# A Mamba-2 scan and a SwiGLU network in one kernel: block 0's scan in chunks of 64, block 1's decays from stored sums, a new order of steps

## The chip, the cores and the metric

The kernel runs on one core of one Trainium2 chip. Its metric is the time of one execution on the device in microseconds (us). The engines are TensorE (PE, with its weight loads PEld), VectorE (DVE), ScalarE (ACT), GpSimd (POOL) and SyncE (SP), which here issues nearly all DMAs.

## What is computed

The reference has two parts. The first is a Mamba-2 scan over x (4 batches, 8 heads, 768 positions, head dimension 32) with decays a and with B and C (state dimension 16). The second is a normed SwiGLU network without biases on the 3072 tokens with 256 features each (model dimension 256, hidden dimension 1536). Cut to what matters:

```
for each chunk of positions:
    cum = cumsum(log(clip(a)))                       # within the chunk
    L   = exp(cum_i - cum_j) for j <= i, else 0
    y   = ((C B^T) * L) x  +  exp(cum) * (C state)
    state = exp(sum log a) * state + sum_j exp(cum_last - cum_j) B_j x_j
X  = y as tokens x 256
xn = X / sqrt(mean(X^2) + 1e-6) * rms_g
out = (silu(xn w_gate) * (xn w_val)) w_out
```

The result of the scan does not depend on the size of a chunk, so a kernel may choose it. The three weight matrices arrive as 64-bit floats; the kernel loads their 16-bit words and makes 32-bit floats of them itself.

## The kernel before

The 3072 tokens are worked in six blocks of 512 (block 0 to 5). A block is two pairs p of two stretches of 128 positions, so blocks 0, 1 and 2 hold the pairs 0 to 1, 2 to 3 and 4 to 5. While TensorE computes the network for one block, the other engines prepare the scan of the next one.

All work is written as small steps, and one string, `order` (line 1269), lists them: `0:gate.2/1` is step gate with the number 2 for block 0, in the PSUM slot 1; a step named `1:S.0` belongs to the table for the later blocks, and acts on the block after the one named (or on the one after that). The list is run through once when the kernel is built, and each step issues its instructions to its engine's queue. So the list is, for each engine by itself, the order in which it works; between engines only the data and the release of buffers order them. DMAs are issued by SP in the same way, each step's DMAs in SP's own order.

The steps that this document speaks of:

- Setup: constants and masks by VectorE and GpSimd (`ident`, `never`, `mid`, `middles` and more, lines 279 to 375); `idle` (line 325), products on zeros at the very start; `bc` and `x` load B, C and x; `aT`, `la0`, `log` turn a and take its logarithms; `c`, `cx`, `ch`, `cc` (lines 426 to 442) make each chunk's whole decay, `d`, `dx` (lines 410 to 420) the decays to and from a chunk's ends.
- Decays L inside a chunk, way one, on TensorE: `mask` (line 457) puts a large negative number above the diagonal, `sums` (line 464) adds differences of sums of logs by small products out of `r` and `parts` (lines 386 to 403: the sums split in three 16-bit parts on VectorE), and `exp` (line 486) takes exponentials. Way two, by loads: `row`, `rowout` (lines 1143 to 1154) store rows of sums in DRAM, `spread` (line 496) loads each row to 64 partitions (128 KB a load), `sub`/`subp` (line 503) subtracts the token's own sum on VectorE/GpSimd, `ex` (line 510) takes exponentials and masks what lies above the diagonal on GpSimd (`causal`, line 491).
- Scores: `turn`, `T`, `Tt`, `Td`, `last` transpose B and C, `g` or `gg` (lines 586 to 616) multiply them, `L` and `L1` (lines 623 to 644) multiply scores by decays on VectorE.
- States: `A` (line 656) adds up B times x on TensorE; `S` (line 671) masks that sum and steps the state from chunk to chunk on VectorE.
- Outputs: `y` (lines 695 and 726) on TensorE; `yt` (line 791) takes them out of PSUM, `sq` (line 769), `ms`, `rs`, `rb`, `xn` (lines 812 to 842) norm them.
- Weights: 18 pieces, `fetch` (line 171) loads one, `pow` (two passes on ScalarE, line 210), `man` and `wt` (VectorE, lines 221 and 227) convert it; six pieces at a time have a buffer.
- Network of block 0: hidden columns 0 and 1 before the norm is known (`early`, line 869, then `norm`, line 882), 2 to 5 by `gate` (line 860), `silu` and `hid`; the rest, and all of the later blocks, by a scheme of fewer products of combined operands: `P` (line 933; seven product steps k for each j), `take`, `C`, `silu`, `hid` (lines 955 to 974), with `cw` and `tx` (lines 909 and 922) for the combinations. The output projection is `o` in block 0 and `O` (line 1060) with `u` and `w` later; `put` stores.

In this kernel block 0 is scanned in chunks of 128 (way one, in four halves `mask.0.0` to `mask.1.1`), and with two output steps `y.0` and `y.1`, one for each pair. Block 1 is scanned in chunks of 64, its decays by way one too (`mask.2`, `mask.3`), its scores with `gg.2` and `gg.3` and its outputs with `y.2` and `y.3`. Blocks 2 to 5 have chunks of 64, decays by way two, one score step, and two output steps each.

PSUM has two pairs of banks for the wide results of blocks 0 and 1 (slots 0 and 1, which `switch` gives to the later pools), a third pair (slot 2) and two single banks (`bank`, line 92). A step that takes a slot waits until the last reader of what was in it is done.

Of the kernel before, what the change touches and what calls it, by code (L numbers as in the profile page):

```python
# [9 lines left out]
FP32 = mybir.dt.float32  # L10
# [10 lines left out]
def kernel(  # L21
# [92 lines left out]
    def load(p, queues=(nc.sync, nc.sync)):  # L114
        br = raw.tile([P, 2, NH, N], FP32, tag="br", name="br")
        st.setdefault(p, {}).update(B=br)
        if p < 4:
            st[p]["C"] = raw.tile([P, 2, NH, N], FP32, tag="cr", name="cr")
        for i, queue in enumerate(queues):
            load_chunk(p, i, queue)  # L120
# [18 lines left out]
    def load_chunk(p, i, queue=nc.sync):  # L139
        b, c0 = divmod(2 * p, NC)  # L140
        sl = slice((c0 + i) * P, (c0 + i + 1) * P)
        for name, src in (("B", B), ("C", C))[0:2 if p < 4 else 1]:
            queue.dma_start(out=st[p][name][:, i], in_=src[b, :, sl, :].rearrange("h s n -> s h n"))

    def load_x(p, queue=nc.sync):
        b, c0 = divmod(2 * p, NC)
        st.setdefault(p, {})["x"] = raw.tile([P, 2, NH, D], FP32, tag="xr", name="xr")
        for i in range(2):
            sl = slice((c0 + i) * P, (c0 + i + 1) * P)
            queue.dma_start(out=st[p]["x"][:, i], in_=x[b, :, sl, :].rearrange("h s n -> s h n"))  # L150
# [59 lines left out]
    def power(k):  # L210
        top, below, dst, shape = fetched[k]
        n = shape[1] * shape[2]
        e = cvt.tile([P, n], FP32, tag="e", name="e", bufs=4)
        g = e.rearrange("p (a b) -> p a b", a=shape[1])
        activation(out=g, in_=top, func=AF.Prelu, scale=-1.0, bias=kinks[:, 0:1],
                   alpha=2.0 ** -40)
        activation(out=g.bitcast(I32), in_=g, func=AF.Prelu, scale=-2.0 ** 59,
                   bias=kinks[:, 1:2], alpha=2.0 ** -40)
        parts[k, "e"] = g.bitcast(I32)
# [7 lines left out]
    def weight(k):  # L227
        top, below, dst, shape = fetched[k]
        e, f = parts.pop((k, "e")), parts.pop((k, "f"))
        nc.vector.tensor_tensor(out=dst.bitcast(I32), in0=f, in1=e, op=ALU.bitwise_or)  # L230
# [13 lines left out]
    later_part = const.tile([P, 1], FP32, name="later_part")  # L244
    third_part = const.tile([P, 1], FP32, name="third_part")
    three = const.tile([P, 1], FP32, name="three")
    head = const.tile([P, NH], FP32, name="head")
    sel = const.tile([P, NH], BF16, name="sel")
    ident16 = const.tile([P, P], BF16, name="ident16")
    whole16 = const.tile([P, P], BF16, name="whole16")  # L250
# [3 lines left out]
    eps = const.tile([P, 1], FP32, name="eps")  # L254
# [3 lines left out]
    NG = 2 * NC * NB + 4  # L258
# [4 lines left out]
    la4 = [early_ones[:, 256 + k * P:256 + (k + 1) * P].rearrange("p (q k h) -> p q k h", q=4, k=4)  # L263
           for k in range(2)]
    mids = const.tile([P, 2, P], FP32, name="mids")
    mid = mids[:, 0]
    first_four = slice(0, 4), slice(0, NH)
# [11 lines left out]
    def whole_chunks():  # L279
        nc.vector.memset(chunk_ones, 0.0)  # L280
        for u, r in enumerate(halves):
            nc.vector.memset(chunk_ones[r, u], 1.0)
# [12 lines left out]
    def of_quarters():  # L295
        nc.vector.tensor_scalar(out=three, in0=part[:, 3:4], scalar1=-1.0, scalar2=1.0,
                                op0=ALU.mult, op1=ALU.add)
        nc.vector.tensor_scalar_add(later_part, part[:, 0:1], -1.0)
        nc.vector.tensor_scalar(out=third_part, in0=part[:, 2:3], scalar1=-1.0, scalar2=None,
                                op0=ALU.mult)  # L300
# [4 lines left out]
    def from_middle():  # L305
        nc.vector.tensor_copy(out=mid, in_=upto)
        nc.vector.tensor_scalar_add(mid[0:HC], mid[0:HC], -1.0)

    def from_middles():
        nc.gpsimd.tensor_copy(out=mid, in_=upto)  # L310
        for r in halves:
            half_of = slice(r.start, r.start + HC // 2)
            nc.gpsimd.tensor_scalar(out=mid[half_of, r], in0=mid[half_of, r], scalar1=-1.0,
                                    scalar2=None, op0=ALU.add)
        minus_mid()

    def mask16():
        for r in halves:
            nc.vector.tensor_copy(out=never16[r], in_=never[r, r])

    def kinks_of_powers():
        for k, v in enumerate((-14336.0, -28672.0 * 2.0 ** 19)):
            nc.vector.memset(kinks[:, k:k + 1], v)
# [18 lines left out]
    def logs_again(g, n):  # L342
        b, c = divmod(g, NC)
        activation(
            out=la4[g // 4][:, g % 4:g % 4 + n],
            in_=la0[:, c:c + n, b * NH:(b + 1) * NH].unsqueeze(2).to_broadcast([P, n, 4, NH]),
            func=AF.Ln)

    def minus_mid():
        nc.gpsimd.tensor_scalar(out=mids[:, 1], in0=mid, scalar1=-1.0, scalar2=None,  # L350
                                op0=ALU.mult)
# [16 lines left out]
        "mid": from_middle, "middles": from_middles,  # L368
        "never16": mask16, "ident16": lambda: nc.vector.tensor_copy(out=ident16, in_=ident),
        "whole16": lambda: nc.vector.tensor_copy(out=whole16, in_=never),  # L370
# [5 lines left out]
        "log": lambda: activation(out=la, in_=la0, func=AF.Ln), "mids": minus_mid,  # L376
# [133 lines left out]
    def exponential(g):  # L510
        L = pair_tile(g)
        activation(out=L, in_=L, func=AF.Exp)
        causal(L)
# [965 lines left out]
```

## Time and profile before

| | us |
|---|---|
| median of 3 runs (388.93 to 391.95) | 389.05 |
| the profiled execution | 389.76 |
| its span, from the first to the last instruction | 388.0 |
| TensorE busy in the span | 382.5 |
| VectorE, ScalarE, GpSimd busy | 277.8, 214.3, 150.1 |
| moved by DMA | 28.04 MB |

The profile is of one execution. Its span starts with the first instruction, and all times in the document count from there. A row of the timeline gives start, duration, engine, line of the kernel, operation and operands with their shapes, and how many like it follow each other; matmuls are pipelined, so the duration of one is longer than the distance to the next one. A 32-bit product is two rows. A row of the groups gives busy us, the mean ns of one instruction, and the idle time before them with what ended it.

### The profile page before, as it was taken

To read this page: it belongs to the slowest core of one execution; us is meant where nothing else is said; L and a number is where in the kernel's file an instruction comes from. 1 tells how busy PE (TensorE), PEld (TensorE's weight loads), DVE (VectorE), ACT (ScalarE), POOL (GpSimd) and SP (SyncE) were. 2 spreads that over 40 slices of the span, in tenths; PEclk is the share of its full clock that TensorE was granted. 3 is DMA by queue.
4 is the path that set the end of the run, shared out by engine and by line. 5 is a ranking of instruction groups with operands and counts; after the bars stand their busy time and mean duration, and the time that the engine had idled before them with its cause. 6 is when DMAs were issued, how large, how long until landed. Compare 5 with 4: busy or idle time off the path is not lost.

```text
span 388.0 us, 9604 instructions
## 1 busy us (share of the span) xinstructions
PE 382.5 (99%) x3805; PEld 330.0 (85%) x3805; DVE 277.8 (72%) x593; ACT 214.3 (55%) x453; POOL 150.1 (39%) x168
## 2 busy tenths in 40 slices
PE   8999999999999999999999999999999999999996
PEld 5676488888888999888899988899888899988995
DVE  6896979876967988669594766868374677454684
ACT  2878677956867272675864244753344571345420
POOL 5022045503693365243568601355611235212231
PEclk9999999999999999999999999999999999999999
DMA  8888988483073404634336112000100001000001
GB/s 91 236 128 233 311 169 179 124 166 30 3 101 87 52 11 96 144 42 100 65 75 85 27 42 42 2 18 19 56 3 2 2 14 48 29 1 0 2 0 56
DMA packets 109940, 28.04 MB, mean 72 GB/s; under 512 B 94824, under 2 KB 107848, under 8 KB 109896
## 3 DMA queue, kind: packets, MB, share of 16 engines
q1 hardware_dynamic: 107816, 27.30, 33.9%
q8 instruction: 30, 0.49, 0.6%
q10 hardware_dynamic: 2080, 0.13, 0.4%
q14 instruction: 14, 0.11, 0.1%
HBM read 23.68 MB, written 3.74 MB: 71 GB/s over the span
## 4 chain that ended last, share of the span: by engine, by line
PE 97%; DVE 1%; ACT 1%; issue 0%; ACTq 0%; DVEq 0%
PE gate L951 29%; PE o L1072 23%; PE val L951 22%; PE o L983 5%; PE gate L865 4%; PE y L736 3%; PE gate L875 2%; PE g L599 2%; PE e L460 1%; PE g L592 1%; PE y L664 1%; PE tp L540 1%; PE e L474 0%; DVE ob L1103 0%; PE idle L328 0%
## 5 line engine op out<-in xcount | busy, mean ns | idle before, releaser
L963 DVE TENSOR_TENSOR c<-val,p 128x512 f32<-128x512 f32 x99 | 67.3, 686 | 49.4 <-PE val L951 35.2
L957 ACT COPY p<-gate 128x512 f32<-128x512 f32 x99 | 56.8, 581 | 61.6 <-PE gate L951 59.3
L951 PE MATMUL gate<-tx,wgv 128*128 128x256 f32 x264 | 65.8, 381 | 0.0
L208 ACT ACTIVATE c<-c 128x256 f32<-128x256 f32 x99 | 40.0, 415 | 39.2 <-DVE c L963 38.9
L976 POOL TENSOR_TENSOR hid<-c 128x256 f32<-128x256 f32 x31 | 23.8, 769 | 89.6 <-ACT c L208 84.9
L951 PEld LDWEIGHTS gate<-tx,wgv 128*128 128x128 f32 x264 | 49.3, 190 | 6.9 <-ACT p L957 0.2
L1103 DVE TENSOR_TENSOR ob<-ob,o 128x128 f32<-128x128 f32 (+1 forms) x90 | 24.2, 297 | 21.7 <-PE o L1072 16.9
L976 DVE TENSOR_TENSOR hid<-c 128x256 f32<-128x256 f32 x68 | 34.0, 513 | 6.7 <-ACT c L208 6.6
L1072 PE MATMUL o<-two,hid 128*128 128x128 f32 x280 | 36.5, 276 | 0.1
L1072 PEld LDWEIGHTS o<-two,hid 128*128 128x128 f32 x280 | 34.5, 192 | 1.1 <-DVE hid L976 0.4
L951 PE MATMUL val<-xn,wgv 128*128 128x256 f32 x132 | 33.7, 381 | 0.0
L951 PE MATMUL val<-tx,sw 128*128 128x256 f32 x132 | 33.5, 380 | 0.0
L951 PE MATMUL val<-xn,sw 128*128 128x256 f32 x132 | 33.3, 381 | 0.0
L951 PE MATMUL gate<-tx,sw 128*128 128x256 f32 x132 | 33.0, 380 | 0.0
L951 PE MATMUL gate<-xn,wgv 128*128 128x256 f32 x132 | 32.7, 380 | 0.0
L493 POOL TENSOR_SCALAR_AFFINE_SELECT L<-L 64x512 f32<-64x512 f32 x32 | 22.8, 713 | 18.1 <-ACT L L208 16.8
L951 PEld LDWEIGHTS val<-xn,wgv 128*128 128x128 f32 x132 | 24.8, 190 | 3.5
L951 PEld LDWEIGHTS val<-tx,sw 128*128 128x128 f32 x132 | 24.9, 190 | 3.4 <-issue 0.2
L951 PEld LDWEIGHTS gate<-tx,sw 128*128 128x128 f32 x132 | 24.8, 190 | 3.4 <-issue 0.2
L951 PEld LDWEIGHTS val<-xn,sw 128*128 128x128 f32 x132 | 24.4, 190 | 3.2 <-issue 0.2
L951 PEld LDWEIGHTS gate<-xn,wgv 128*128 128x128 f32 x132 | 24.4, 190 | 3.1
L208 ACT ACTIVATE u<-gate 128x256 f32<-128x256 f32 (+1 forms) x37 | 14.6, 402 | 18.2 <-PE gate L951 15.3
(202 smaller groups left out, 702.6 us busy)
## 6 DMA issues: line engine op xcount, KB each, us to landing
L<-rowd SPq DMA_DIRECT2D x32, 128.0 KB, 3.3
xr<-in_x_dram SPq DMA_DIRECT2D x24, 128.0 KB, 3.6
out_dram<-ob SPq DMA_DIRECT2D x24, 128.0 KB, 2.4
wr<-in_moe_w_out_dram SPq DMA_DIRECT2D x6, 511.5 KB, 6.3
wr<-in_moe_w_gate_dram SPq DMA_DIRECT2D x5, 511.5 KB, 5.4
wr<-in_moe_w_val_dram SPq DMA_DIRECT2D x5, 511.5 KB
br<-in_B_dram SPq DMA_DIRECT2D x23, 64.0 KB, 2.6
dT<-rowe SPq DMA_DIRECT2D x10, 128.0 KB
```

Of the source, the lines that this page charges most:

```text
L208: nc.scalar.activation(**operands)
L493: nc.gpsimd.affine_select(out=L[r], in_=L[r], pattern=[[0, L.shape[1]], [1, HC]], compare_op=ALU.is_ge, fill=0.0, base=0, channel_multipli ...
L599: nc.tensor.matmul(out=g[u, P * i:P * i + P].rearrange("p (t m) -> p t m", t=2), lhsT=T[r, i, 0, u], rhs=T[r, i, 1:3, u], start=(first and ...
L736: nc.tensor.matmul(out=y[2 * k + u][rows, (2 * n + i) * HC:(2 * n + i + 1) * HC], start=(k, u, rows.start) not in opened, stop=True, skip_ ...
L865: nc.tensor.matmul(out=gv[:, k], lhsT=w[:, t, fs], rhs=xns[0][:, t], start=(t == 0), stop=(t == 1))
L951: nc.tensor.matmul(out=dst[:, half[w]], lhsT=lhsT, rhs=rhs, start=(k in (1, 2, 5) and w == 0), stop=True, skip_group_check=True)
L957: nc.scalar.copy(out=t, in_=Xs[j])
L963: nc.vector.tensor_tensor(out=t, in0=Zs[j], in1=a, op=ALU.add)
L976: engine.tensor_tensor(out=hid[:, 2 * j + c // 10 - 1, c % 10 - 1], in0=u, in1=src[:, half[1]], op=ALU.mult)
L983: nc.tensor.matmul(out=o, lhsT=hid[:, f, k // 2, (k % 2) * P:(k % 2 + 1) * P], rhs=wo[:, f], start=opens, stop=(f == NF - 1), skip_group_c ...
L1072: nc.tensor.matmul(out=Os[blk, b][:, place * P:(place + 1) * P], lhsT=hidden_or_sum(u)[:, g], rhs=rhs, start=(blk, b) not in opened, stop= ...
L1103: nc.vector.tensor_tensor(out=o, in0=o, in1=src, op=ALU.add if what[0] == "+" else ALU.subtract)
```

## The change

Three things change together.

First, block 0 is scanned in chunks of 64 like the rest. Its decays still come from TensorE, but with the narrow masks and sums that block 1 had (`mask.0`, `mask.1`, `sums.0`, `sums.1`); its scores are one step (`g.0`), its state sums are one step for both pairs (`AA.0`), with `Sn` to mask them and seven states instead of four, and its outputs are one step, `y.0`. All later blocks too have one output step in place of two, with the state sums for the next block behind it:

```
-    def outputs(p, pair, after, n=0):
+    def outputs(blk, pair):
...
+        def between():
+            for j in range(4):
...
+        def within():
+            for j in range(4):
...
+        if blk == 0:
+            within()
+            between()
+        else:
+            between()
...
+            within()
+            if blk + 1 < NBLK:
+                next_additions()
```

Second, block 1's decays come by way two: `spread.4` to `spread.7` in two loads each (one for each half of the partitions), `subp` on GpSimd, `ex`, and `ca` for the mask. `mask.2`, `mask.3`, their sums, `r.1` and `parts.1` go away, and so do the wide mask, the sums over all 128 positions in `d` and `c`, and the two filler products ahead of `c`:

```
-            for u in range(2):
-                n = sum(v == u for i, v in chunks)
...
+    def spread(g, u):
         b, c = divmod(g, NC)
         o = (c * BH + b * NH) * HC
...
+        r = halves[u]
+        nc.sync.dma_start(out=pair_tile(g)[r].rearrange("p h m -> p (h m)"),
+                          in_=rowv[u, o:o + NH * HC].partition_broadcast(HC))
```

Third, many steps are cut finer (`pow` in its two passes, `parts` in four, `norm`, `xn`, `sq`, `yt`, `rs`, `middles`), B and C share five buffers in place of three each, x has four in place of three, and the whole list is in a new order. The parts of the new list that the prediction speaks of, the steps of one stretch as they stand there:

```
0:idle.7 ... 0:mask.0/0 0:sel 0:middles.0 0:bc.0 0:x.0 0:aT ... 0:la0 0:log ... 0:turn.0 0:Tb.0 0:T.0
0:c/2 0:r.0 0:row.1 0:parts.0.0 0:cx 0:mask.1/1 0:fetch.1 0:rowout.1 0:rowe.1 0:d 0:dx 0:tok 0:tokout
0:turn.1 0:T.1 0:parts.0.1 0:ch 0:cc 0:parts.0.2 0:parts.0.3 0:sums.1 0:exp.1 0:x.1 ... 0:Tb.1 0:fetch.0
...
0:spread.4.1 0:spread.5.1 0:spread.5.0 0:fetch.3 0:fetch.2 0:bc.2 0:sums.0 0:exp.0 0:g.0/2 0:L1.0.3
0:L1.0.2 0:L.0 0:last.1 0:pow.1.0 0:Tl.1 0:AA.0/0 0:Sn.0.0 0:Sn.0.1 0:S.0.0 ... 0:S.0.6 0:y.0/1
...
0:early.0.1/0 0:early.0.0 ... 0:ms.0 0:rs.0.0 0:rs.0.1 0:wt.3 0:xn.0.1 0:xn.0.0 0:turn.2 0:T.2 0:Tt.2.0
0:norm.0.0 0:tx.0.2 0:subp.4 0:ca.5.1 0:pow.2.1 0:early.1.0/2 0:ex.4 0:ca.4.1 0:ca.4.0 0:bc.3 0:scale.3
0:early.1.1 0:norm.1.0 0:norm.1.1 0:silu.0 ... 0:turn.3 ... 0:pow.5.0 0:wt.2 0:gate.2/1
...
0:gate.3/0 0:g.1/1 0:x.2 0:x.3 0:ex.7 0:AA.1/2 0:Sn.1.1 0:Sn.1.0 0:ca.7.0 0:ca.7.1 0:fetch.7 0:L.1
0:S.1.4 0:L1.1.3 0:S.1.0 0:hid.1 0:L1.1.2 0:man.7 0:cw.0.1 0:S.1.1 0:silu.3 0:pow.7.0 0:pow.7.1
0:fetch.6 0:pow.6.0 0:man.6 0:pow.6.1 0:S.1.2 0:wt.6 0:S.1.5 0:table.1 0:wt.7 0:S.1.6 1:cwp.2.0 0:fetch.9
0:pow.9.0 0:hid.3 0:S.1.7 0:cw.1.1 0:cwp.3.0 0:cw.3.1 0:cwp.3.3 0:fetch.8 0:switch.0 0:man.8 0:gate.4/2
0:silu.4 0:pow.9.1 0:gate.5/1 0:silu.5 0:P.1.3 0:take.1.3 0:P.6.3 0:pow.8.0 0:pow.8.1 0:bc.5 0:hid.5
0:hid.4 0:cw.3.2 0:fetch.11 0:cw.1.2 0:man.9 0:switch.1 0:P.2.3 0:cwp.0.3 0:take.6.3 0:P.7.3 0:wt.8
0:wt.9 0:P.1.4
```

The parts of the old list for the same stretch, block 0's wide products and what stands between them, are: `early.0`, `ms.0`, `mask.2`, `sums.3`, `sums.2`, `turn.2`, `turn.3`, `early.1`, `gate.2`, `gg.2`, `gate.3`, `gate.4`, `A.2`, `gate.5`, `y.2`, `P.2.3`, `P.1.3` and so on, with `gg.3` and `y.3` among the P steps.

938 lines of the change are left out of this document (436 added, 502 removed).

## The prediction

> **What bounds the kernel now.** I read the page first (busy times), then the waits of TensorE, then three stretches, then the early timeline.
>
> ```profile
> span 388.0 us, 9604 instructions
> PE 382.5 (99%) x3805; PEld 330.0 (85%) x3805; DVE 277.8 (72%) x593; ACT 214.3 (55%) x453; POOL 150.1 (39%) x168
> ```
> ```profile
> PE idle L328 <- DVE warm L354: 1.1, 1, 1.1
> PE y L705 <- DVE S L686: 0.5, 1, 0.5
> PE o L1072 <- DVE ob L1103: 0.4, 1, 0.4
> ```
> TensorE is busy 382.5 of 388.0 us, and its waits are three, 2.0 us in all, two of them at the start. So after the start the time is TensorE's work. The start is different: the columns below are the stretch, its length, busy us and instructions of PE, PEld, DVE, ACT and POOL, then granted clock, DMA share and GB/s.
>
> ```profile
> 0.00:22.57 22.57, 20.69 (x254) 14.09 (x254) 17.67 (x53) 13.52 (x26) 6.50 (x19) 1.00 0.86 157
> 22.57:48.57 26.00, 26.00 (x205) 14.83 (x203) 21.50 (x48) 19.59 (x31) 3.73 (x5) 1.00 0.91 237
> 48.57:63.31 14.74, 14.74 (x353) 12.45 (x352) 12.43 (x27) 11.06 (x25) 8.07 (x11) 1.00 0.89 171
> ```
> ```profile
> 22.57 3.62 PE L875 MATMUL gate<-yt,wgv 128*128 128x256 f32 x16
> ...
> 26.02 1.02 PE L816 MATMUL ms<-sq,mean 128*128 128x512 f32 x2
> 26.88 0.59 PE L460 MATMUL e<-never,ident 128*128 128x512 bf16 x2
> ...
> 28.49 0.44 PE L540 MATMUL tp<-ident,br 128*128 128x128 f32 x2
> ...
> 29.42 3.69 PE L875 MATMUL gate<-yt,wgv 128*128 128x256 f32 x16
> ```
> The first wide product (step early.0) starts at 22.57. Before it lies block 0's scan, small products fed in turn by VectorE and ScalarE; from it to 63.31 block 0's weights are still converted and VectorE is busy 83%, DMA 90%. Two questions decide: does early.0 start sooner, and is TensorE still fed behind it?
>
> **The change, part by part.**
>
> *Block 0's scan (the start).* TensorE loses the wide masks, half of the decay sums, a second sum of logs, and two of the four output bursts. But VectorE's queue gives the outputs, and it is about as long as before. Its rows:
>
> ```profile
> L224 DVE TENSOR_SCALAR m<-wr 128x512 int32<-128x512 uint32 x18 | 8.6, 477 | 0.5 <-DMA wr<-in_moe_w_gate_dram 0.3
> L230 DVE TENSOR_TENSOR wgv<-m,e 128x512 int32<-128x512 int32 x12 | 8.5, 714 | 0.5 <-ACT e L208 0.2
> L638 DVE TENSOR_TENSOR L<-g,L 128x1024 f32<-128x1024 f32 x4 | 4.7, 1219 | 1.1 <-PE g L592 1.1
> L632 DVE TENSOR_TENSOR L<-g,L 128x512 f32<-128x512 f32 x8 | 5.3, 681 | 0.7 <-POOL L L493 0.7
> L688 DVE SCALAR_TENSOR_TENSOR S<-S,fcol,A 128x64 f32<-128x64 f32 x36 | 10.6, 296 | 1.0
> L678 DVE TENSOR_TENSOR A<-y,tmask 128x128 f32<-128x128 f32 x15 | 3.7, 281 | 0.4 <-PE y L664 0.2
> L886 DVE TENSOR_TENSOR u<-gate,sq 128x512 f32<-128x512 f32 x2 | 1.4, 683 | 0.0
> L898 DVE TENSOR_TENSOR hid<-u,gate 128x512 f32<-128x512 f32 x4 | 2.7, 682 | 1.1 <-ACT u L208 1.0
> L920 DVE TENSOR_TENSOR sw<-sw,wgv 128x256 f32<-128x256 f32 x4 | 1.7, 414 | 0.0
> L847 DVE SCALAR_TENSOR_TENSOR xn<-yt,gcol,sq 128x512 f32<-128x512 f32 x10 | 7.0, 745 | 0.8 <-DMA sq<-roots 0.8
> L525 DVE TENSOR_TENSOR Bd<-br,d_sb 128x256 f32<-128x256 f32 x11 | 5.6, 512 | 0.2 <-DMA br<-in_B_dram 0.2
> ```
> ```profile
> 3.10 0.22 DVE L307 TENSOR_SCALAR mids<-mids 64x128 f32<-64x128 f32 x1
> ...
> 8.75 0.69 DVE L559 TENSOR_TENSOR T<-tp,tmask 128x512 f32<-128x512 f32 x1 [0.57 <-PE tp L540]
> ```
> (Columns: line, engine, form, count; then busy us, mean ns; then idle before it.) The product of scores and decays falls from four steps of 1.22 to one of 1.22 and two of 0.68: 2.3 us less. Against it stand seven states (0.30 each) for four, two masked additions of twice L678's width (at most 0.56 each; I take 0.42) for two of 0.28, four small steps on the constants that come over from POOL (0.2 each, as L307's), and the second turned block, which is now masked here (L559's 0.69): 0.9 + 0.3 + 0.8 + 0.7 = 2.7. So 17.7 busy us become 18.1. The waits in that queue (22.57 - 17.67 = 4.9, of them 0.9 before its first step) have no clear reason to shrink: the sum over heads (cc) now stands between the row parts and waits for POOL; the first transposes stand on TensorE ahead of the chunk sums, so a late load of B or C holds those; the last transposes wait for banks that L1.0.2 and L1.0.3 free. I take the start of early.0 as unchanged, with bounds of 21.0 (the waits fall by 2) and 24.0.
>
> The clock beside it:
>
> ```profile
> 2.80 1.01 PE L460 MATMUL e<-whole,ident 128*128 128x512 bf16 x2
> ...
> 7.68 0.60 PE L460 MATMUL e<-whole,ident 128*128 128x512 bf16 x2
> ```
> The same pair takes 1.01 us early and 0.60 later: TensorE begins slow, and here it has been fed without a gap up to then. In the new order it has gaps (masks wait for a constant that POOL makes last, the transposes for B), and the two filler products ahead of the chunk sums are gone. [...]
>
> *Products saved behind early.0.* Block 1's masks and sums go: 28.49 - 26.88 = 1.6 us. Its two score products become one, and each block's two output bursts become one:
>
> ```profile
> 36.48 1.11 PE L599 MATMUL g<-T 32*64 32x128 f32 x32
> ...
> 54.60 0.69 PE L599 MATMUL g<-T 32*64 32x128 f32 x32
> ```
> ```profile
> 174.02 1.89 PE L951 MATMUL val<-tx,sw 128*128 128x256 f32 x8
> 175.74 1.03 PE L951 MATMUL gate<-tx,wgv 128*128 128x256 f32 x4
> 176.70 0.49 PE L736 MATMUL y<-T,S 32*64 32x64 f32 x32
> ...
> 178.22 1.13 PE L951 MATMUL gate<-tx,wgv 128*128 128x256 f32 x4
> 179.19 1.89 PE L951 MATMUL val<-xn,sw 128*128 128x256 f32 x8
> ```
> The second score product (0.69 and its turn in and out) saves about 0.8. Eight wide products take 1.72 (174.02 to 175.74), so four take 0.86; the four before a burst take 0.96 and the four after it 0.97. So a burst costs 0.2 for entering and leaving, and I add as much for the changes of shape inside: 0.4 each in blocks 1 to 4 and 0.2 in block 5, whose bursts stood together: 1.8. Saved: 1.6 + 0.8 + 1.8 = 4.2 (bounds 3.4 and 5.0).
>
> *New waits of TensorE.* The new order puts four places where TensorE's next product stands behind VectorE steps that cannot come earlier, since VectorE takes its list in order.
> (A) gate.2 needs wt.2, and wt.2 stands behind norm.1.0 and norm.1.1, which wait for early.1. From the end of early.1: 0.68 + 0.71, less the one transpose in between (0.45, half of 28.49 to 29.42): 0.95 at least. From the first norm on, the queue between the roots and wt.2 is two xn, three norms, tx, a scale and wt.2 (1.49 + 2.05 + 0.41 + 0.51 + 0.71 = 5.2; tx as L920), against 3.45 (22.57 to 26.02) and two transposes, 4.35, on TensorE; with the roots' two passes over 128x512 on ScalarE (0.63 each, by the exponentials' row below) the wait would be 2.1. I take 1.6.
> (B) gate.4 takes the banks of the additions AA.1, and TensorE has nothing between: two masked additions and their hand-over, 0.95 (0.6 to 1.2).
> (C) P.1.3 takes the banks of gate.3, which hid.3 frees. From gate.4's start VectorE has L.1 and two L1 (2.6), six states (1.8), hid.1 and hid.3 (1.4), two man (1.0), one cw (0.4), wt.6 and wt.7 (1.4): 8.6, against two gates of 3.45 on TensorE: 1.7. P.6.3 needs three steps more (1.1) against one product step of 0.86: 0.2.
> (D) P.1.4 needs wt.8, seven steps on (0.48 + 0.68 + 0.68 + 0.41 + 0.41 + 0.48 + 0.71 = 3.85), against three product steps, 2.6: 1.2.
> Together 1.6 + 0.95 + 1.9 + 1.2 = 5.65 (from 2.5, if VectorE's shorter forms and idle time in front carry part of C and D, to 7). Behind D, until block 1's first product, VectorE has some 18 us of steps (three quarters of them the C, S, wt and hid rows) against 21 us of products, so it catches up.
>
> *Block 1's decays.* Eight loads of 128 KB, four subtractions and eight masks on POOL, four exponentials on ScalarE:
>
> ```profile
> 56.17 3.94 SPq L500 DMA_DIRECT2D L<-rowd x6
> ```
> ```profile
> L493 POOL TENSOR_SCALAR_AFFINE_SELECT L<-L 64x512 f32<-64x512 f32 x32 | 22.8, 713 | 18.1 <-ACT L L208 16.8
> L506 POOL TENSOR_TENSOR L<-L,tok 128x512 f32<-128x512 f32 x8 | 8.7, 1087 | 2.6 <-DMA L<-rowd 2.5
> L208 ACT ACTIVATE L<-L 128x512 f32<-128x512 f32 x16 | 9.9, 628 | 0.1
> L202 ACT ACT_TABLE_LOAD x11 | 14.1, 1283 | 1.0 <-PEq L1463 0.8
> ```
> SP's queue gains 8 x 0.66 = 5.3 us of issues among the weights; POOL 4 x 1.09 + 8 x 0.71 = 10.1 us in a stretch where it is busy 3.7 of 26. Both end at L.1, which stands before hid.1, wt.6 and hid.3 in VectorE's queue. I count nothing: by those rows the last mask ends about when VectorE gets there, at 42 us (22.57, four wide groups of 3.45, ms.0, two transposes, A, g.1 and AA.1). If that cover is gone, each us is paid in full. ScalarE changes its table 30 times where it did 22 (8 x 1.28 = 10.3 us), hidden while it is idle 45%. The staged steps, packed constants and renamed buffers issue the same instructions: nothing.
>
> **The sum.** 0 - 4.2 + 5.65 = +1.45: 388.0 becomes 389.45. The profiled execution took 389.76, that is 1.76 beyond its span and 0.7 above the median of the runs, 389.05; on that scale 389.05 + 1.45 = 390.5.
>
> **The rivals.**
> *The saved work stays saved.* If VectorE reaches gate.4 with its queue emptier than I count, C and D vanish, and if the start gains its 1.5, only A's floor and B are left: 389.05 - 1.5 - 4.2 + 1.9 = 385.2, and 384.4 with 5.0 saved. For it: VectorE is busy only 21.5 of 26.0 us in that stretch before; against it: A and B follow from the order alone.
> *Block 1's loads come late (slower).* The place is L.1. DMA is at 0.91 there, and eight more loads lie among the weights; if the last of them lands 3 us later than I count, hid.3 and wt.6 are 3 us later and so is P.1.3: 393.4. It decides from the point where TensorE's idle time before P.1.3 passes 4 us. Against it: block 1's x loads and dT lie behind them and have room.
> [...]
>
> **How the numbers follow.** The sum's own range is 387 to 393 (2.5 to 7 of waits, 1.5 at the start, 0.8 of savings). Chances: it 0.45, saved work 0.30, late loads 0.15, cold start 0.10. About 1%, 3.9 us, is what a measurement of this kernel can tell from no change: below 385.2 half of the first rival and a tail of the sum, 0.20; above 392.9 most of the other two and a tail of the sum, 0.30; within, 0.50. The range from 384 to 396 leaves out about 2 in 10, on both sides.
>
> **What would show it.** Right: early.0 within 1.5 us of 22.57; idle time of TensorE before gate.2, gate.4, P.1.3 and P.1.4 of 1 to 2 us each, released by VectorE (wt, A, hid); none of note after 63 us; one output burst per block. Wrong: TensorE idle under 2 us in all, or a DMA or POOL as releaser, or rows at double length after 8 us.

## The result and the profile after

The changed kernel takes 412.93 us (median of 4 runs, 407.69 to 420.28), the kernel before 389.0 beside it (388.93 to 391.95): a ratio of 1.051, 95% interval 1.039 to 1.063. The forecast was 390.5 in a range from 384 to 396. The profiled execution took 414.44 us with a span of 412.7, against 388.0 before, so 24.7 us have to be found in it. The ratio compares the two faster of the four runs with the kernel before, and the profiled execution is one of the two slower. The scatter is news too: 12.6 us between runs where there were 3.

Five lines of the page of the kernel after: its first two, the granted clock in 40 slices, one queue, and the sums of the chain that ended last:
```profile
span 412.7 us, 9867 instructions
PE 384.1 (93%) x3939; PEld 333.6 (81%) x3939; DVE 268.5 (65%) x580; ACT 223.8 (54%) x453; POOL 154.9 (38%) x173
PEclk9969979699999999999999999999999999999999
q8 instruction: 31, 0.51, 0.5%
PE 90%; issue 5%; DVE 3%; DMA 1%; ACT 1%; SPq 0%; DVEq 0%
```
TensorE has slightly more to do than before (384.1 for 382.5, and 134 more matmuls in number), the granted clock falls to 0.6 and 0.7 in three slices, and 5% of the chain is "issue": time in which TensorE waited for nothing that the profile shows. The waits of TensorE, engine, line and releaser first, then sum, number and longest:
```profile
PE y L611 <- issue: 7.0, 3, 4.2
PE y L654 <- issue: 6.1, 3, 3.1
PE A L611 <- issue: 3.5, 1, 3.5
PE gate L793 <- DVE wgv L226: 2.1, 1, 2.1
...
PE gate L793 <- DVE A L623: 1.0, 1, 1.0
...
PE gate L881 <- ACT p L887: 0.7, 1, 0.7
```
Seven stands, 16.6 us, all inside output bursts (y) or the additions (A), none of which has a releaser. Below them are the waits that the prediction had listed: wt.2 before gate.2 (2.1) and the banks of the additions before gate.4 (1.0). The last line is a wait of 0.7 before P.6.3, for ScalarE. Three stands in the timeline of TensorE (start, length, form, and idle time ahead of it in brackets; from here on a product is a row of the timeline, so a 32-bit product counts twice): in the output burst of block 0 (with early.0 behind it), in the additions for block 1, and in the burst of block 1:
```profile
21.35 0.42 PE L654 MATMUL y<-L,xr 64*32 64x64 f32 x21 [3.09 <-issue]
...
24.79 6.17 PE L805 MATMUL gate<-yt,wgv 128*128 128x256 f32 x16
...
50.61 0.46 PE L611 MATMUL A<-xr,Bd 64*32 64x64 f32 x15 [3.51 <-issue]
52.07 9.60 PE L793 MATMUL gate<-xn,wgv 128*128 128x512 f32 x16 [1.00 <-DVE A L623]
...
68.74 0.85 PE L654 MATMUL y<-T,S 32*64 32x64 f32 x56
69.52 1.48 PE L654 MATMUL y<-L,xr 64*32 64x64 f32 x128
70.80 0.33 PE L611 MATMUL y<-xr,Bd 64*32 64x64 f32 x10
75.29 1.10 PE L611 MATMUL y<-xr,Bd 64*32 64x64 f32 x54 [4.16 <-issue]
76.32 2.07 PE L881 MATMUL gate<-tx,sw 128*128 128x256 f32 x4
```
In the last of them, after ten of 64 products of one kind and between two that read the same tiles, TensorE stands 4.2 us. Then its wide products, four in 1.03 us elsewhere, take 2.07. Windows around it (the stretch, its length, busy us of PE, PEld, DVE, ACT and POOL, granted clock, DMA share, GB/s) show the clock beside it:
```profile
71.00:75.30 4.30, 0.14 (x12) 0.01 (x2) 0.22 (x1) 0.38 (x1) 2.08 (x3) 0.87 0.44 112
76.30:81.00 4.70, 4.70 (x14) 3.78 (x12) 1.29 (x3) 3.95 (x8) 1.27 (x1) 0.50 0.01 3
```
Little else works in the stand either (GpSimd 2.08 of 4.30 us); behind it the granted clock is 0.50 for 4.7 us.

What the seven have in common comes out when TensorE's instructions (matmuls, weight loads and the 67 of its sequencer) are counted in the trace: each stand lies behind instruction 193 plus a multiple of 256, and each holds or follows one 16 KB transfer of the queue that the page calls "q8 instruction" (31 x 256 = 7,936; TensorE has 7,945, and 0.51 MB over them is 64 bytes each). "Border" is the start of the instruction 256 places earlier, that is, the border before the one at which TensorE stands:
```
stand from   border at   transfer          next product
 18.04        15.90       17.40 -  19.70    21.35
 46.88        38.70       48.17 -  49.17    50.61
 70.91        69.58       72.70 -  73.78    75.29
154.30       152.86      153.35 - 154.23   155.80
178.15       176.79      177.46 - 178.46   179.66
220.24       218.98      219.82 - 220.69   222.03
285.00       283.53      284.36 - 285.58   286.98
```
The product behind a stand comes 1.2 to 1.7 us after the end of its transfer. In the kernel before no stretch of 256 instructions between two borders took less than 3.6 us (137.46 to 141.06); in the joined bursts one runs through in 1.3 to 1.5 before the stand. With the time from each matmul to the next set against what is usual for its form, the spans divide so (us):
```
kernel        span   stands   half-speed rows   waits and turns over 0.15   rest
before        388.0    0          0.2                 8.3                  379.5
after         412.7   18.1        5.7                13.1                  375.8
```
The stands are longer here than in the list of waits (18.1 for 16.6) because they run from start to start, while idle time runs from the modelled end of a matmul. What counts as usual moves the other columns by up to 2 us: read row against row, the three slow stretches alone come to 7.4 (6.17 for 3.62, 9.60 for 7.11, and 4.98 for about 2.6 behind block 1's burst). So the change did save 3.7 us of products, or up to 5.5, and added 4.8 of waits, near the forecast's totals (4.2 and 5.65); 18.1 us of stands and 5.5 or more of half-speed rows are what the prediction did not have.

### The profile page after: what moved, and what is told of

Its sections match the earlier page's. It is cut to its first block, busy times and chain, and to the rows that moved or that the text cites. A ratio compares the mean times of both kernels' runs of the same rounds, so it can differ in the third digit from the quotient of the medians.

```text
span 412.7 us, 9867 instructions
## 1 busy us (share of the span) xinstructions
PE 384.1 (93%) x3939; PEld 333.6 (81%) x3939; DVE 268.5 (65%) x580; ACT 223.8 (54%) x453; POOL 154.9 (38%) x173
## 4 chain that ended last, share of the span: by engine, by line
PE 90%; issue 5%; DVE 3%; DMA 1%; ACT 1%; SPq 0%; DVEq 0%
PE gate L881 28%; PE o L1002 22%; PE val L881 21%; PE o L913 5%; PE gate L793 4%; PE y L654 3%; PE g L573 2%; PE gate L805 1%; PE y L611 1%; DMA br<-in_B_dram 1%; DVE L L595 1%; PE r_ps L1071 0%; PE ms L743 0%; ACT sq L203 0%; DVE xn L780 0%
## 5 line engine op out<-in xcount | busy, mean ns | idle before, releaser
L906 POOL TENSOR_TENSOR hid<-c 128x256 f32<-128x256 f32 x31 | 22.7, 739 | 86.2 <-ACT c L203 86.2
L906 DVE TENSOR_TENSOR hid<-c 128x256 f32<-128x256 f32 x68 | 31.7, 473 | 13.3 <-ACT c L203 12.9
L1002 PE MATMUL o<-two,hid 128*128 128x128 f32 x280 | 37.6, 277 | 0.1
L479 POOL TENSOR_SCALAR_AFFINE_SELECT L<-L 64x512 f32<-64x512 f32 x40 | 27.4, 693 | 24.6 <-ACT L L203 15.4
L881 PE MATMUL val<-xn,wgv 128*128 128x256 f32 x132 | 34.6, 388 | 0.0
L881 PE MATMUL val<-xn,sw 128*128 128x256 f32 x132 | 34.3, 386 | 0.0
L976 POOL TENSOR_TENSOR s<-hid 128x512 f32<-128x512 f32 x13 | 18.1, 1398 | 28.1 <-DVE hid L906 24.5
L881 PEld LDWEIGHTS val<-xn,sw 128*128 128x128 f32 x132 | 24.7, 195 | 3.5 <-DVE c L893 0.2
```

Of the source, the lines that this page charges most:

```text
L479: nc.gpsimd.affine_select(out=L[r], in_=L[r], pattern=[[0, L.shape[1]], [1, HC]], compare_op=ALU.is_ge, fill=0.0, base=0, channel_multipli ...
L881: nc.tensor.matmul(out=dst[:, half[w]], lhsT=lhsT, rhs=rhs, start=(k in (1, 2, 5) and w == 0), stop=True, skip_group_check=True)
L906: engine.tensor_tensor(out=hid[:, 2 * j + c // 10 - 1, c % 10 - 1], in0=u, in1=src[:, half[1]], op=ALU.mult)
L976: engine.tensor_tensor(out=hidden_or_sum(o), in0=hidden_or_sum(in0), in1=hidden_or_sum(in1), op=ALU.add if in1[0] == "+" else ALU.subtract)
L1002: nc.tensor.matmul(out=Os[blk, b][:, place * P:(place + 1) * P], lhsT=hidden_or_sum(u)[:, g], rhs=rhs, start=(blk, b) not in opened, stop= ...
```

## The experiments

Two theories. **F**: TensorE's own instructions are late. By the table they come in blocks of 256, one transfer of 16 KB each. That the next block is asked for about when one is entered is my assumption; what the table shows is that the seven transfers began 0.5 to 9.5 us after the border, and that the product behind the stand came 2.9 to 11.9 us after it, where a burst runs through 256 in 1.3 to 1.5. **H**, the rival: a hand-over inside the burst that the profile does not show (banks, states, decays). F ties a stand to a count of instructions, H to an operation.

### The bursts cut in two
```
- 0:P.1.4 ... 0:x.5 0:y.1/2 0:sq.1.1 ... 0:P.6.4
+ 0:y.1.0/2 0:P.1.4 ... 0:x.5 0:P.6.4 0:y.1.1 0:sq.1.1 ...
(blocks 2 to 5 in the same way, around two to five steps)
```


> The changed kernel with the output bursts of blocks 1 to 5 cut in two, two to four wide products or projections between the halves; everything else as changed. Theory F (TensorE's own instructions come late): the trace after has seven places where TensorE stands for 1.5 to 4.4 us with nothing to wait for, each after a multiple of 256 of its instructions, and each ends 1.2 to 1.7 us after a 16 KB transfer of the instruction queue. A burst runs 256 instructions in about 1.45 us, and a transfer is asked for only when the block before is entered and takes about 3.4 us in all. Halves with 1.8 to 3.5 us between them leave that time: the five stands in bursts (4.38 + 1.49 + 1.51 + 1.80 + 1.98 = 11.2) and the half-speed rows behind the first of them (about 2.6) go, each cut costs 0.2 to 0.4: about 400 us (397 to 404) against 412.9. Rival H (a hand-over that the profile doesn't show, of banks, states or decays inside the burst): the same product stands for as long wherever the burst is cut: 412 to 414.

Measured: 405.0 us (401.7 to 408.8), 1.037 of before (1.031 to 1.043). The timeline of block 1's burst:
```profile
59.88 0.85 PE L659 MATMUL y<-T,S 32*64 32x64 f32 x56
60.66 0.86 PE L659 MATMUL y<-L,xr 64*32 64x64 f32 x64
61.45 1.13 PE L891 MATMUL gate<-xn,wgv 128*128 128x256 f32 x4
...
65.10 0.86 PE L659 MATMUL y<-L,xr 64*32 64x64 f32 x64
65.77 0.85 PE L611 MATMUL y<-xr,Bd 64*32 64x64 f32 x64
```
The same 248 products with four groups of four wide ones between the halves, and no stand. Of the five stands in bursts one is left, 0.9 us in block 4; the one at the start stays (2.8). For F, against H. The time fell by 8 us and not by 13: the halves were put where their operands were not ready, which cost some 3 us of new waits behind VectorE and ScalarE. Part of the fall is not the edit's: the stand in block 1's additions is gone too, although the list is that of the changed kernel up to block 1's outputs. Its border is passed at 38.8 us here and at 38.7 there, but its transfer began at 39.53 and not at 48.17, and the 16 wide rows behind it take 7.11 us instead of 9.60. So that stand is in the one profiled execution and not in the other, with the same list ahead of it, and some of the scatter of the changed kernel may be this; no run here separates it.

### 98 more instructions early
```
- 0:idle.7 ... 0:aT 0:whole.1
+ 0:idle.7 0:tick.29 ... 0:aT 0:tick.20 0:whole.1
+ def tick(n):
+     for k in range(n):
+         nc.tensor.matmul(out=ps["idle"][0:32, 0:32], lhsT=warm[0:32, 0:32],
+                          rhs=warm[0:32, 0:32], start=True, stop=True)
```


> The changed kernel with 49 matmuls of 32x32 by 32 more before 5 us, where TensorE is idle: 98 more instructions, no other difference. F: every stand moves 49 matmuls earlier in its burst, since it sits at a count of instructions and not at an operation: in block 1's output burst after about 89 of the 128 products of decays and tokens instead of after 10 of the additions. At the start the second block of instructions is asked for at about 14 us instead of 15.9, so the stand of 3.3 us at 18 shrinks to 1 to 2; the stand of 3.7 us in block 1's additions goes with its half-speed rows (2.9), since the border then falls between the score products and them, 22 us after the one before. 404 to 408 us. H: the stands stay at the same products and as long; 412 to 414.

Measured: 406.9 us (403.4 to 408.9), 1.044 of before (1.037 to 1.050). Block 1's burst and block 5's:
```profile
65.20 0.85 PE L659 MATMUL y<-T,S 32*64 32x64 f32 x56
65.97 1.10 PE L659 MATMUL y<-L,xr 64*32 64x64 f32 x89
67.92 0.65 PE L659 MATMUL y<-L,xr 64*32 64x64 f32 x39 [0.84 <-issue]
68.36 0.85 PE L616 MATMUL y<-xr,Bd 64*32 64x64 f32 x64
```
```profile
279.50 0.91 PE L659 MATMUL y<-T,S 32*64 32x64 f32 x64
280.34 1.48 PE L659 MATMUL y<-L,xr 64*32 64x64 f32 x128
```
The stand sits behind 89 of the 128 products, as forecast, where it sat behind ten of the additions. In block 5, where it sat behind 172 of 192 products (64 and 108), the second border is now at 123 and the first lies ahead of the burst: no stand. The additions of block 1 have none either. H can say none of this, and the time lies in F's range. Seven stands are left all the same, 10.1 us by the waits: two at the start, 0.8, 2.1, 1.4 and 2.0 in the bursts of blocks 1 to 4, and 1.1 before a step of norm sums. The start missed: the stand at 18 us did shrink, to 1.8, but a border now falls into the score products of block 0, with a stand of its own (0.8), and the granted clock is low from there:
```profile
16.20:29.85 13.65, 10.84 (x263) 8.51 (x264) 9.43 (x23) 6.31 (x14) 2.30 (x3) 0.50 0.76 195
```
In the changed kernel it falls only at 22.95. So early.0 comes at 26.98 instead of 24.79.

### Both together
The two edits above in one kernel.

> Both edits together: bursts of blocks 1 to 5 cut in two and 98 more instructions early. F: only a stand of 1 to 2 us at the start and rests of at most 0.5 us in a burst are left: about 392 us (388 to 396). H: 412 to 415. If it comes below 389, the order without its stands was worth what the rival 'the saved work stays saved' gave.

Measured: 404.4 us (403.9 to 404.7), 1.038 of before (1.036 to 1.040), 12 above F's number. No burst of blocks 1 to 5 has a stand, but the start has two (1.1 and 2.1, TensorE's waits put them to "issue"), the wait before gate.2 is 2.1 as in the change, and the cuts keep their waits. F's part came out; my arithmetic for the start did not: there the changed kernel runs through the instructions from 82 to 869 in 13.3 us, 10 without the stand, over three borders, and with 98 more ahead over four, so moving them moves the stand. The granted clock is 0.50 from 15.4 to 29.1 us here, and early.0 comes at 27.07.

### Two bursts joined in the kernel before
```
- 2:y.0 2:P.2.3 ... 3:S.0 ... 2:P.4.3 2:y.1 3:S.1
+ 2:P.2.3 ... 2:P.4.3 2:y.0 2:y.1 3:S.0 3:S.1
(and block 4's in the same way)
```


> The kernel before with the two output bursts of block 3 put together, and those of block 4, as the change does; nothing else. F: where two multiples of 256 fall within a joined burst, TensorE stands 1.5 to 2.0 us there; two bursts, less 0.2 to 0.4 saved for each: about 392 us (389.5 to 393.5) against 389.05, and the profile shows idle time without a releaser inside the joined bursts. H, and the prediction's term for the bursts: 0.2 to 0.4 us saved for each and no stand: 388.3 to 388.7.

Measured: 399.5 us (398.9 to 400.4), 1.026 of before (1.024 to 1.029), above both. TensorE's waits:
```profile
PE y L664 <- DMA xr<-in_x_dram: 2.5, 2, 2.1
...
PE y L736 <- issue: 1.5, 1, 1.5
```
Block 4's joined burst stands 1.5 us where F puts it. In block 3's the additions waited 2.1 us for the inputs x, probably because the move had put the burst that frees their room behind their loads. The border there is at 176.49 and the transfer ends at 178.64, so the wait, over at 180.15, covers what F would have put there. Another 2.0 us were waits for ScalarE. The size of a join can't be read from this run; the direction for block 4 can.

### A run that reads only still data, and the same under load
```
+ 5:run.40        (320 matmuls of the additions' form on the weights, behind the last step)
+ 5:more.5 ... 5:more.10 5:run.40    (six weight transfers ahead of it)
```
The results of the added products and the data of the added transfers are not used.

> The kernel before, and behind its last projection a run of 320 small matmuls on weights that have long been still (the form of the additions, 4 TensorE instructions each, 1,280 in all; their results are not used). F: after the one or two blocks of 256 instructions that lie ready, each further 256 take the time of a fetch, about 3.4 us (request, a transfer of about 1 us, 1.2 to 1.7 us until use), although the engine could run them in about 1.45: three or four stands of about 2 us, at multiples of 256, each with a transfer of the instruction queue inside; the run takes 12 to 16 us. H: nothing is handed over in this run, so there is no stand: about 7.3 us.

> As the run of 320 small matmuls behind the kernel before, but with six weight transfers (about 3 MB, their data not used) issued just ahead of it, so that the data queues are full. F, with the fetch queued behind data as the trace after suggests (request to transfer up to 9.5 us with the queues full, 0.8 to 1.0 with them empty): stands of 3 to 6 us as long as the data flow, about 2 behind them. F without that queueing: stands of about 2 us throughout, as in the run without loads. H: no stand.

Measured: 403.1 and 406.7 us in one run each, 14.0 and 17.6 over before. First without, then with the transfers:
```profile
388.29 1.47 PE L1247 MATMUL run<-wo 64*32 64x64 f32 x128 [1.74 <-issue]
392.02 2.04 PE L1247 MATMUL run<-wo 64*32 64x64 f32 x128 [2.26 <-issue]
395.47 2.04 PE L1247 MATMUL run<-wo 64*32 64x64 f32 x128 [1.41 <-issue]
399.20 0.85 PE L1247 MATMUL run<-wo 64*32 64x64 f32 x35 [1.69 <-issue]
```
```profile
388.54 1.47 PE L1247 MATMUL run<-wo 64*32 64x64 f32 x128 [1.75 <-issue]
395.83 2.04 PE L1247 MATMUL run<-wo 64*32 64x64 f32 x128 [5.82 <-issue]
```
This is the direct measurement. Nothing is handed over here, and behind the first 221 rows TensorE stands after every 128, that is 256 instructions. A block takes 3.73, 3.45 and 3.73 us (388.29 to 392.02 and so on), of which the products, from the first start to the last, fill 1.3, and 1.7 from 390.4 us on, where the granted clock is 0.50. Under load one block took 7.29 (388.54 to 395.83): the views of the queues show 882 data packets and no transfer of instructions from 388.6 to 393.3. Its transfer ran from 393.46 to 394.43, while data still flowed. Without load the transfer began 1.1 to 1.2 us after the border at 388.29, under load 4.9 after the one at 388.54. H falls; F holds, and here the transfer came later with data in the queues.

### Transfers of the start moved away
```
- 0:man.1 0:spread.4.1 0:spread.5.1 0:spread.5.0 0:fetch.3 0:fetch.2 0:bc.2 ... 0:spread.4.0 ... 0:fetch.4
+ 0:man.1 0:fetch.3 ... 0:rowout.0 0:spread.4.1 0:spread.5.1 0:spread.5.0 0:fetch.2 0:bc.2 0:spread.4.0 0:fetch.4
```


> The changed kernel with five transfers of the start (the spread loads of chunks 4 and 5, a quarter of the next weights, one load of B and C, the fifth piece of the weights) moved on SyncE's list behind the store of the row sums, some 10 us later; TensorE's list is the same. F with queueing: the data queues are nearly empty from about 16 us, so the second fetch begins within 1 us of its request and is used by 19 to 20 us; the stand at 18 us falls from 3.3 to 1.0 to 1.7, the first wide product from 24.8 to 22.5 to 23.2, and fewer of its rows run at half speed. Without queueing the stand stays at 3 us or more. H: it stays. The delayed loads may lengthen later waits.

Measured: 416.5 us in one run, inside the scatter of the changed kernel. The stand at 18 us shrinks from 3.1 to 2.25 and early.0 comes at 23.96, earlier by as much; its transfer still began 2.2 us after its border, while the queues moved 351 and 360 GB/s from 16 to 18 us. Later, norm sums waited 6.0 us for a step of GpSimd that stands behind a subtraction whose load had been delayed. That is at most half of what F expected of the start, and no version of use.

### The kernel before with its borders moved
```
- 0:idle.7
+ 0:idle.5 0:tick.30
```


> The kernel before with two of its seven warming matmuls exchanged for 30 of 32x32 by 32, of about the same time: 56 more TensorE instructions, nothing else. In the kernel before only block 5's output burst (384 instructions in one piece) could hold two multiples of 256, and it holds one, after 75 of its 192 matmuls. F: 28 matmuls more move it to 47, and a second to 175: TensorE stands about 2 us there with nothing to wait for, and the kernel takes 390.5 to 391.2 us. H: no stand, 388.8 to 389.5.

Measured: 395.5 us (393.7 to 397.8), 1.018 of before (1.013 to 1.023). Block 5's burst:
```profile
299.82 0.72 PE L742 MATMUL y<-L,xr 64*32 64x64 f32 x49
302.24 0.42 PE L742 MATMUL y<-L,xr 64*32 64x64 f32 x15 [1.70 <-issue]
```
Fifty-six instructions more, 298 us earlier, and a burst that had run through stands behind 177 of its 192 products; the forecast was 175. Six rows behind it run at half speed. That is 3.2 us of the profile's 5.1; a wait of 1.0 at 67 us and a start 1.0 later make the rest. The waits put the one at 67 us down to ScalarE, but it lies at a border as well, and the instruction there starts at 68.21, 1.5 us after the end of a transfer (65.42 to 66.70): by its place it is a stand too. The later start stays open, and so does why the time lies 4 us above F's range.

### The change, cut better, two waits shortened
```
- 0:early.1.1 0:norm.1.0 ... 0:wt.2 0:gate.2/1      - 0:g.1/1 0:x.2 0:x.3 0:ex.7 0:AA.1/2
+ 0:early.1.1 0:wt.2 0:norm.1.0 ... 0:gate.2/1      + 0:x.2 0:x.3 0:AA.1/2 0:g.1/1 0:ex.7
(bursts cut as before, the halves of blocks 3 to 5 at later places)
```


> The changed kernel with its bursts cut as before but at places where the halves' operands are ready, one weight step (wt.2) ahead of the two norms, and block 1's additions ahead of its score products, so that these cover the hand-over of the banks. F with the prediction's terms A and B: against the first cut version the waits that the cuts made (about 3.5 us) go, the wait before gate.2 falls from 2.2 to about 0.8, that before gate.4 from 1.15 to 0.2, and the one stand left in a burst (1.1) goes: 394 to 398 us. What is left over the kernel before is the start (one stand of 2 to 3.3 us, half-speed rows behind it, about 2.5). If it comes no lower than 401, the waits were only moved.

Measured: 402.3 us (400.9 to 402.9), 1.033 of before (1.030 to 1.035), above the limit that I had set for "only moved". TensorE's waits:
```profile
PE y L659 <- issue: 3.2, 2, 3.1
PE gate L891 <- DVE hid L838: 1.5, 1, 1.5
PE gate L803 <- DVE wgv L226: 1.3, 1, 1.3
```
The wait for gate.2 fell from 2.0 to 1.3 and that for gate.4 is gone, but P.1.3 now waits 1.5 for hid.3: the prediction's wait C. P.1.3 starts at 55.00, and it started at 55.21 without a wait in the first cut version, so what A and B gave up came back as C. By the division used above: stands 3.3, half-speed rows 3.2, waits and turns 16.5, rest 377.5. Against 375.8 in the change, cutting costs 1.7: what joining was counted to save. So the cuts took away 14.8 us of stands, not all of them by their own doing (the additions have none here either), and 2.5 of half-speed rows, and gave back 3.4 of waits and 1.7 of products: 12.2 of the span. Of the 12.5 us that are left over the kernel before, stands and half-speed rows are 6.3 and waits 8.2, less 2.0 of products.

### Block 1's decays alone, three times
In the kernel before, block 1's masks, sums and sums of logs go, and eight loads with their subtractions, exponentials and masks come; 24 small matmuls keep two borders out of block 5's burst.
```
- 0:mask.3/1 0:r.1 0:parts.1 0:mask.2/2 0:sums.3 0:sums.2 0:exp.3 0:exp.2
+ 0:rowout.0 0:spread.4 0:spread.5 0:spread.6 0:spread.7 ... 0:subp.4 0:subp.5 0:sub.6 0:sub.7 0:ex.4 0:ex.5 0:ex.6 0:ex.7 0:table.1
second:  spread.4 and 5 ahead of rowe.0 and rowout.0, ex.6 and 7 behind silu.2, 8 more small matmuls ahead of gate.4
third:   spread.4 and 5 behind rowout.0, then dT.3, then spread.6 and 7; 26 small matmuls in idle gaps before 5 us instead of the others
```


> The kernel before with one part of the change alone: block 1's decays from the stored sums, spread by eight loads (subtractions on GpSimd and VectorE), its masks, its 72 spreading products and the sums of logs behind them taken out; 24 small matmuls are put in after block 0's projections so that block 5's burst holds one multiple of 256 of the instructions and not two. The prediction counted the saving as 1.6 us (1.8 with the sums of logs, less 0.3 for the filling) and the eight loads as hidden: 387.2 to 388 us. Its rival (block 1's loads come late) and a delay of weights by the loads: 391 to 394, with TensorE idle behind VectorE, GpSimd or a weight between 30 and 60 us. F expects no stand by count in either.

> The part alone once more, with what the run before it showed mended: chunks 4 and 5 are loaded ahead of the stores of block 0's sums and their exponentials stand ahead of the first silu, those of chunks 6 and 7 behind silu.2 (two more table loads on ScalarE), and 8 more small matmuls ahead of gate.4 move the multiples of 256 so that no burst holds two of them. Against the run before: the 6.9 us in which the score products stood behind VectorE and ScalarE go, the stand of 1.9 us and its half-speed rows go: 387 us (386 to 389), 0.5% below the kernel before, if the exponentials of chunks 6 and 7 are hidden; 389 to 392 if they hold up ScalarE's silu or block 1's decays.

> The part alone a third time: in the run before, TensorE stood 6.4 us in the first score products of block 1 for a product of VectorE whose operand, dT.3, is loaded behind the spread loads on SyncE's list. Here dT.3 goes ahead of the loads of chunks 6 and 7, right behind those of 4 and 5, and the small matmuls that keep the multiples of 256 apart (26 of 32x32 by 32) are issued in two idle gaps before 5 us instead of later. The queue is the cause: the 6.4 us and the half-speed rows behind them (1.2) go, and the part alone takes 387.5 to 389.5 us, as the saving of 1.6 us less what is left of waits. If the loads themselves are what comes late (the rival of the prediction), TensorE waits there or at block 1's outputs for 2 us or more: 391 to 396.

Measured: 398.9, 399.9 and 398.1 us; 1.024 (1.022 to 1.027), 1.026 (1.023 to 1.029) and 1.022 (1.019 to 1.025) of before. All three forecasts were too low. The products did go (in the first, early.0 comes at 20.74 instead of 22.57), but TensorE then stands 6.7, 6.4 and 5.2 us in block 1's first score products. What VectorE waits for at that place, from 28 to 42 us, in the first, second and third:
```profile
DVE L L506 <- DMA L<-rowd: 4.4, 2, 3.7
DVE T L573 <- DMA dT<-rowe: 2.7, 2, 2.4
```
```profile
DVE T L573 <- DMA dT<-rowe: 6.6, 2, 4.3
DVE m L224 <- DMA wr<-in_moe_w_val_dram: 1.7, 1, 1.7
```
```profile
DVE m L224 <- DMA wr<-in_moe_w_val_dram: 5.1, 1, 5.1
DVE T L579 <- DMA dT<-rowe: 2.2, 1, 2.2
```
The kernel before has one such wait there, 3.1 us in two pieces for dT, and TensorE does not stand behind it. Each time I moved the load that was late ahead, and the next in SyncE's list became the late one: the spread rows, then dT.3, then a piece of w_val. In three versions of the old order the eight loads were not hidden. The first and the third also had a stand in block 1's second burst (1.7 and 2.2), each at a border, which F's forecast had left out: in the first the border before it is only 3.3 us old, and in the third the transfer began 4.7 us after its border. No version of this series, and none of the change, came below the kernel before.

## Why the prediction was wrong

*The step that failed* is the price of a joined burst: "a burst costs 0.2 for entering and leaving, and I add as much for the changes of shape inside: 0.4 each in blocks 1 to 4 and 0.2 in block 5 ...: 1.8" saved. The turns are saved, as the 1.7 us that cutting costs again shows. But a joined burst of about 512 instructions (384 in block 5) holds two borders with 1.3 to 1.5 us of products between them, where a block took 2.9 to 3.5 us from its border to the product behind the stand in blocks 2 to 5, with the queues nearly empty (DMA share 0.02 to 0.27), 3.45 to 3.73 in the run without transfers, and 5.7 in block 1 with them full (1.07 from 69.58 to 72.70). Five bursts cost 4.4 + 1.5 + 1.5 + 1.8 + 2.0 = 11.2 us of stands and 2.4 of half-speed rows. The rows that I had quoted priced products by their time and never by their number.

*The start*: "start of early.0 unchanged", bounds 21.0 to 24.0; it came at 24.79. VectorE's list, which I had weighed, is not what delayed it: less the stand of 3.3 us at 18 the row would stand at 21.5, an estimate that the run with moved transfers supports for its first 0.8 us. Scanning in chunks of 64 makes 869 TensorE instructions ahead of early.0 instead of 516, and the data queues are busy there (DMA share 0.80 from 13.0 to 24.8 us, 197 GB/s). Ten of the 16 rows of early.0 then ran at half speed (6.17 us for 3.62; early.1 takes 3.62 again). The granted clock was 0.50 from 22.95 to 29.78. To that the "cold start" of the forecast's chances (0.10) came nearest; its price was my estimate, and no trace of the kernel before shows it (the granted clock is 1.00 in all of its span). What the runs show is a clock that fell 1.6 us after the end of a stand of 3.3 us, and in the two versions with 98 more instructions early one that fell at 15.4 and 16.2 us, with early.0 at 27.07 and 26.98.

*The additions of block 1*: not in the prediction; a stand of 3.7 us with 0.5 clock behind it (9.60 us for 7.11). Here the border was 8 us old; the transfer began at 48.2, when the data queues had run nearly empty (DMA share 0.99 from 38.7 to 46.0 us, 0.36 from 47.2 to 48.17). The cut versions with the same start do not have this stand.

*Waits A and B*: 1.6 and 0.95 forecast, 2.1 and 1.0 measured, released by wt and A as said. *C and D*: 1.9 and 1.2 forecast; nothing before P.1.3 and P.1.4, and 0.7 before P.6.3 for ScalarE's `take`, not for VectorE. TensorE came to gate.4 10 us later than I had counted, which gave VectorE time. In the better cut version, where it came 6 us earlier again, C is there with 1.5. So C lay under the stands and under A and B; no run showed D. That the total of the waits came out near the forecast is in part luck.

*Block 1's decays as nothing*: true in the new order, whose list puts their loads ahead of the stores and weights (TensorE has no wait for them in block 1); false in the old one, where TensorE stood 5 to 7 us. The cover that I named, VectorE's arrival at L.1, was not the limit; what lay behind the loads on SyncE's list was.

*The rival "saved work stays saved"* was right about the work, 3.7 us, and that C and D would vanish, but by the stands and not by an emptier queue; it did not decide the time. The better cut version speaks against the order itself too: with one long stand left, it is still 12.5 us of span over the kernel before, 8.2 of them waits.

The signs named in advance, "rows at double length after 8 us" and early.0 off by more than 1.5, did show that the prediction fails. None named time without a releaser.

In the kernel before the shortest 256 instructions took 3.6 us from border to border, and TensorE did not stand there. A burst issues 256 in 1.3 to 1.7 us; from the border to the product behind the stand it then took 2.9 to 3.7, and 7.29 with the data queues full.

## What to carry to other kernels

Small matmuls have a second price, their number: two instructions for each pass (3,939 matmuls and as many weight loads in the kernel after), four for a product of f32 (the 320 products added behind the kernel before are 640 rows), and 256 of them took 3.45 to 3.73 us here in the run that reads only still data, and 5.4 to 7.3 while large transfers filled the queues (11.9 once, in the additions). So spread bursts of small products between wide ones rather than joining them, look at time put to "issue" inside a burst before any other wait, and count instructions when it sits between two alike products. A wait that is removed shows the next one in the same list: the loads of block 1 took three names in three runs.

## What the runs showed of the hardware

- With data in the queues instruction transfers mostly came later: in bursts with the queues nearly empty one began 0.5 to 1.2 us after its border and was used 1.2 to 1.7 us after its end; with full ones it began 0.7 us (additions, bursts cut in two), 3.1 us (burst of block 1), 4.9 us (run under load) and 9.5 us (additions) after it. One in the kernel after began 12 us late (border at 50.61) though the queues were idle for the first 6 of them (DMA share 0.01 from 50.61 to 56.6, 1.04 from there to 62.6), and that stays open.
- Between wide products 11 of the 31 transfers of the kernel after begin up to 2.7 us before TensorE reaches their border, so the start of that instruction on the engine is not what sets them off; these runs do not show what does.
- The place of a border is set by everything ahead of it: 56 instructions before 5 us put a stand at 302 us. The two kernels, with nearly the same products in the same order, differ by 5.1 us of span (393.1 for 388.0).
- Half-speed rows (426 to 428 ns from one to the next in early.0, where 216 is usual) stood behind idle time here, though not behind a fixed length of it: after the three stands of 3.3 to 4.4 us 6 to 10 rows ran at half speed, after those of 1.5 to 2.0 in the kernel after none, and after the one of 1.9 in the kernel before with moved borders six. The low stretches of the granted clock are 6.83 us long in the kernel after (22.95 to 29.78, 50.26 to 57.09, 74.15 to 80.98) and 3.41 in the kernel before with moved borders (302.37 to 305.78). The first length is twice the second; what sets them, and with them the spread, these runs do not show.
